# Second sequence's queries and keys prepared sooner and ahead of V, and the last weight part decoded where it was loaded

## The chip, the cores and the metric

The kernel runs on 1 core of a Trainium2 chip. The metric is the device time of one execution in microseconds (us). A core has five engines that work side by side, each through a queue of its own, in order: PE (matmuls), DVE and ACT (elementwise work on vectors), POOL (gathers and some elementwise work) and SP (which issues most DMAs). They wait for each other through semaphores.

## The reference

Block-sparse attention over 4 sequences of 8 heads, 768 tokens and 64 channels, and behind it a feed-forward layer of two matmuls over all 3072 tokens.

```python
mask = np.abs(blk_i - blk_j) <= 1            # blocks of 32 tokens
mask |= (blk_i == 0) | (blk_j == 0) | (blk_i == n_blocks - 1) | (blk_j == n_blocks - 1)
mask |= sampled                              # three random key blocks for each query block
attn = softmax(where(mask, scale * q @ k.T, -1e9))
x = (attn @ v).transpose(0, 2, 1, 3).reshape(B * S, H * D)      # 3072 x 512
h = x @ w_in                                 # 512 x 2048, given as float64
out = np.maximum(0.01 * h, h) @ w_out        # 2048 x 512, given as float64
```

## The kernel before

**Numbers in two halves.** Queries, keys, V, the probabilities, x and the weights are each split into a high and a low float16 half, and products are made from two or three matmuls. Each operand is first scaled by a power of two; for that it is squared and summed (on ACT with `square`, for the weights on PE with `squares`), the sum goes through PE once more (`scale_sum`: rows named q_sum, k_sum, v_sum, wi_sum, wo_sum) and a few small DVE instructions make the scale (`scale_of`).

**Attention.** The work goes in steps, 192 in all: for each of 4 sequences, 3 items of 256 queries, in each 4 tiles of 64 queries, for each tile 4 pairs of heads. Steps 0 to 47 are sequence 0, and step 48 is the first of sequence 1. Names carry these numbers: s_0_2_3_1 is sequence 0, item 2, tile 3, head pair 1, so step 45 (rows of the order leave out the first number in places). A step has scores on PE (`scores`, L714), the masked softmax on DVE and ACT (p, L723 and L735), the probabilities' two halves (pp, `unit_high` on ACT L762, `unit_split` on DVE L783), a transpose by DMA for two pairs together (pt, L788), and the product with V on PE (av, `pair_av`, L815). p has 4 buffers, pp and pt 3 each: pp of a pair can be written once the pair three before has been transposed. Tiles 1 to 11 of a sequence read their sampled keys and values from gathers: `gather_k` copies them out of kt on POOL (kg), and `gather_v` by indirect DMA out of scr, where V's halves are written.

**Side work.** Before a sequence starts, its keys (`prep_k`, four head pairs), V (`prep_v`) and queries (`prep_q`, halves of 128 queries) are prepared. These are generators; `side_step` advances them once a step by a quota, queries first and the others in the order in which they were started. `prep_q` squares on ACT, sums on PE, splits on ACT and DVE (qa), transposes by DMA into qs (L599), and copies qs with its halves swapped into qxs (L601, L602). The first scores of a sequence need qs, qxs and kt of head pair 0. kt has 2 buffers; sequence 1's kt takes the place of sequence 0's.

**Weights.** They are given as float64 and decoded on the chip. They come in 8 parts, w_in and w_out in turn (wi0, wo0, ... wi3, wo3; parts 0 to 7), each of 4 chunks of 128 x 512. `load_w` loads raw words into a free place (`raw_for`); `decode` makes float32 in W from them with one ACT and three DVE instructions (L363 to L367); `finish` squares a part on PE (`squares`, L201), makes its scale and writes the two halves over W (L430 and L435). Parts 6 and 7 go chunk by chunk (groups of one chunk), through three half places in wbuf. Both decode into the last slot of W, so part 7 is decoded only when part 6 has been split, and its own halves go through a temporary in wbuf (L425, L426, L428).

**The feed-forward layer.** h (`ffn_h`, L850) are groups of 24 matmuls, then ACT L856, DVE L859 and L863 and POOL L864 make g, and o (`ffn_o`, L877) are 12 matmuls a group. The first two items go weight part by weight part, as parts come in; the others once all weights are there. From step 48 on h groups are handed out by a table of due steps.

**What sets the order.** A scheduler puts the instructions of each engine into a fixed order, by priorities and by buffers. PE's results of h, of all sums and of all squares share 3 banks of PSUM (`bank`, tag h), taken in the order of the program: what takes a bank early in the program stands early on PE.

Of the kernel before, what the change touches and what calls it, by code (L numbers as in the profile page):

```python
# [12 lines left out]
BF16 = mybir.dt.bfloat16  # L13
F32 = mybir.dt.float32
I32 = mybir.dt.int32
AF = mybir.ActivationFunctionType
# [3 lines left out]
P = 128  # L20
# [39 lines left out]
    "side": 1.2,  # L60
    "side0": 1.6,
    "spair": 1,
    "spread": 8,
# [9 lines left out]
def tile_block_sparse_attention_ffn(  # L73
# [99 lines left out]
    def together(emits):  # L173
# [15 lines left out]
        "p a b c -> p (a b c)").bitcast(F32)[:, :P]  # L189

    def squares(parts, name, fl):

# [3 lines left out]
        pb = bank(f"{name}_sq")  # L196
        blocks = [t.bitcast(BF16).rearrange("p (n l) -> p n l", l=2)[:, c:c + P, 1]
                  for t in parts for c in range(0, t.shape[1], P)]
        begin = len(nc.cur_bb.bb.instructions)
# [119 lines left out]
    wlast = wbuf.bitcast(I32).rearrange("p (c l) -> p c l", l=2)  # L319
    used, busy = {}, set()  # L320
    wtmp = [wbuf[:, WI * i:WI * (i + 1)] for i in range(2)]
    W16 = W.rearrange("p a b c -> p (a b c)").bitcast(F16).rearrange("p (a b l c) -> p a b l c", a=2 * NQ, b=NP, l=2)
# [4 lines left out]
    def raw_for(part, w, n):  # L327

        if w == 1:
            free = [("w", i) for i in range(3)]  # L330
        else:
            free = [a for a in range(4, 2 * NQ) if a >= part + 2 and (
                a == 4 or part and all((0, hp) in kready for hp in range(NP)))] + ["w"]
# [8 lines left out]
        if a == "w":  # L342
            return wlast[:, :2 * WI], keys(a)
        return half(wlast, a[1]) if w == 1 else wraw[a - 4], keys(a)

    def load_w(g):
# [9 lines left out]
        nc.sync.dma_start(out=raw.rearrange("p (c x) l -> p c (x l)", c=g.w), in_=src.bitcast(I32))  # L356
        behind(begin, last_sp.get("p"))

        def decode():
# [15 lines left out]
    def prep_weights():  # L375
# [3 lines left out]
        for n in range(NQ):  # L379
            for k_, kind in enumerate(("wi", "wo")):  # L380
# [4 lines left out]
                for c in range(0, NP, w):  # L385
                    g = Group()
                    g.part, g.w, g.n = i, w, NP * i + c
                    g.d3, g.d16 = W[:, at, c:c + w, :], W16[:, i, c:c + w]
                    g.d = g.d3.rearrange("p c x -> p (c x)")
                    g.src = (w_in[c * P:(c + w) * P, n * WI:(n + 1) * WI] if k_ == 0  # L390
                             else w_out[(n * PER + c) * P:(n * PER + c + w) * P, :])
# [25 lines left out]
        def finish(n, kind, gs):  # L417
            inv, s = scales(squares([g.d for g in gs], f"{kind}{n}", "w"), 1, f"{kind}{n}", keep=f"{kind}{n}", fl="w")
            invs[kind, n] = inv
            yield 1  # L420
            for i, g in enumerate(gs):
                hi, lo = g.d16[:, :, 1, :], g.d16[:, :, 0, :]
                if (n, kind) == (NQ - 1, "wo"):
                    tmp = wtmp[i % 2].unsqueeze(1)
# [21 lines left out]
        for n, kind, gs in parts:  # L446
            for i, g in enumerate(gs):
                load(CFG["ahead"])
# [5 lines left out]
            before = (n, kind, gs)  # L454
            if gs[0].part >= 2 * NQ - 2:
                yield from finish(*before)
                before = None
# [497 lines left out]
    def side_step(amount):  # L955

        quota[0] = min(quota[0] + amount, 2 * amount)
        for key in sorted(flows, key=lambda a: a[0] != "q"):
            if quota[0] <= 0:
# [179 lines left out]
    for u in units:  # L1139
# [5 lines left out]
        if step == 6 or step % 8 == 3 and step > 8:  # L1145
            get_q((step + 5) // 8 + 1)
        if step % 8 == CFG["q_at"] % 8:
            start_q(step // 8 + (2 if CFG["q_at"] < 8 else 1))
        if nb < B:
            g = it.j * 16 + ui  # L1150
            t = g - (CFG["k_at"] if b else CFG["k_at0"])
            every = CFG["k_every"] if b else 5
            if t % every == 0 and 0 <= t // every < NP:
# [26 lines left out]
        for w in CFG["ord1" if step >= CFG["ord1_at"] else "ord"]:  # L1180
# [49 lines left out]
            elif w == "p":  # L1230
                side_step(CFG["side0"] if step < 16 else CFG["side"])
                gather_step(2)
# [83 lines left out]
```

## Time and profile before

| | |
|---|---|
| time, median of 3 runs | 850.7 us (850.25 to 853.37) |
| the profiled execution | 851.52 us |
| its span, first to last instruction | 849.8 us |
| PE busy (share of the span) | 749.3 us (88%) |
| DVE busy | 595.5 us (70%) |
| ACT busy | 507.6 us (60%) |
| POOL busy | 352.8 us (42%) |
| mean granted clock of PE | 0.955 |

Busy time is that of instructions, not of their waits. A row of the timeline has its start, its length in us, the engine, the line, what is written and read, how many instructions were merged, and in brackets how long the engine was idle ahead of it and what ended that. SPq is SP's queue of DMA issues: the length is that of the issue, not of the transfer. PE's granted clock is the share of full clock that the throttle let through.

### The profile page before, as it was taken

How to read it: one execution, taken by the hardware profiler on the slowest of the kernel's cores; microseconds unless marked ns; L12 is line 12 of the kernel's file. 1: busy time of each engine (PE TensorE's matmuls, PEld its weight loads, DVE VectorE, ACT ScalarE, POOL GpSimd, SP SyncE). 2: the span in 40 equal slices, each digit the busy share in tenths (PEclk: the TensorE clock that was granted, in tenths of full speed). 3: DMA queues.
4: the chain of work that ended last, by engine and by line, in shares of the span. 5: the costliest groups of instructions: out<-in, count | busy, mean ns of one | idle time of the engine just before them, and what ended most of it. 6: DMA issues, size and time to landing. Idle time of an engine off the chain costs nothing.

```text
span 849.8 us, 20081 instructions
## 1 busy us (share of the span) xinstructions
PE 749.3 (88%) x7140; PEld 500.6 (59%) x7140; DVE 595.5 (70%) x1595; ACT 507.6 (60%) x1199; POOL 352.8 (42%) x472
## 2 busy tenths in 40 slices
PE   1666675857798999999999999998999999999997
PEld 1455543545465666666666666665666666667664
DVE  5768889898777976867777777678666776651221
ACT  5757678776445766767566667675657556551211
POOL 0218356433233464646343455454244545332221
PEclk9977778989799999999999999999999999999999
DMA  9979289998756999996969999969586766662000
GB/s 198 273 218 247 73 176 240 245 260 147 168 131 106 175 213 190 203 179 146 197 154 154 196 182 186 202 130 204 119 155 150 125 149 139 125 129 35 26 1 25
DMA packets 312004, 135.33 MB, mean 159 GB/s; under 512 B 279774, under 2 KB 292063, under 8 KB 311903
## 3 DMA queue, kind: packets, MB, share of 16 engines
q1 hardware_dynamic: 305262, 113.59, 67.2%
q0 software_dynamic: 6640, 20.45, 9.3%
q8 instruction: 56, 0.92, 0.5%
q14 instruction: 46, 0.37, 0.2%
HBM read 65.58 MB, written 12.58 MB: 92 GB/s over the span
## 4 chain that ended last, share of the span: by engine, by line
PE 70%; DMA 12%; DVE 10%; issue 3%; ACT 2%; SPq 2%; POOL 0%; POOLq 0%; ACTq 0%; DVEq 0%
PE h L850 27%; PE o L877 26%; PE s L714 8%; PE av L815 7%; DMA pt<-pp 3%; DMA wbuf<-in_moe_w_out_dram 2%; DMA qxs_q<-qs_q 2%; DMA qs_q<-qa_q 2%; DVE p L723 2%; DVE pp L783 2%; PE turn L773 2%; DVE W L365 1%; DVE W L435 1%; DVE W L367 1%; PE q_sum L135 1%
## 5 line engine op out<-in xcount | busy, mean ns | idle before, releaser
L877 PE MATMUL o<-W,g 128*128 128x512 f16 x1152 | 270.9, 381 | 6.4 <-DVE ob L898 4.2
L850 PE MATMUL h<-x,W 128*128 128x256 f16 x2304 | 274.2, 277 | 0.2 <-DVE x L833 0.2
L850 PEld LDWEIGHTS <-W 128*128 128x128 f16 x2304 | 225.0, 100 | 37.7 <-issue 3.9
L864 POOL TENSOR_TENSOR g<-ht,g 128x512 f16<-128x512 f32 x96 | 116.9, 1217 | 304.5 <-DVE g L863 254.6
L735 ACT ACTIVATE p<-p,mx 128x384 f32<-128x384 f32 x208 | 126.2, 607 | 158.7 <-DVE mx L723 123.0
L877 PEld LDWEIGHTS <-g 128*128 128x128 f16 x1152 | 108.7, 98 | 125.6 <-issue 10.8
L656 POOL COPY kg<-kt 128x256 f16 x264 | 135.0, 540 | 45.0 <-issue 15.4
L783 DVE SCALAR_TENSOR_TENSOR pp<-p,r,pp 128x384 f16<-128x384 f32 x188 | 120.4, 666 | 24.9 <-ACT pp L762 23.6
L762 ACT ACTIVATE pp<-p,r 128x384 f16<-128x384 f32 x188 | 104.2, 604 | 23.9 <-DVE r L747 10.2
L723 DVE CUSTOM_DVE_ANT_0 p<-s,em,nsc 128x384 f32<-128x384 f32 x176 | 102.0, 608 | 19.8 <-PE s L714 17.1
L683 POOL DMA_INDIRECT vg<-scr,rows x88 | 91.3, 1037 | 50.4 <-issue 20.3
L859 DVE SCALAR_TENSOR_TENSOR ht<-ht 128x512 f32<-128x512 f32 x96 | 67.8, 706 | 53.3 <-ACT ht L856 52.7
L815 PE MATMUL av<-pt,vg 128*64 128x128 f16 x2112 | 82.1, 226 | 10.1 <-DMA pt<-pp 9.6
L815 PEld LDWEIGHTS <-vg 128*64 128x64 f16 x2112 | 73.4, 114 | 27.4 <-issue 21.7
L714 PE MATMUL s<-kg,qs_q 128*64 128x384 f16 x352 | 66.2, 351 | 25.0 <-DVE mx L723 22.7
L856 ACT ACTIVATE ht<-h,gd 128x512 f32<-128x512 f32 x80 | 53.8, 672 | 57.3 <-PE h L850 54.7
L714 PEld LDWEIGHTS <-qs_q 128*64 128x64 f16 x416 | 27.0, 111 | 79.2 <-issue 53.7
L714 PE MATMUL s<-kg,qxs_q 128*64 128x384 f16 x352 | 64.0, 343 | 5.4 <-DMA qxs_q<-qs_q 5.4
L747 DVE RECIPROCAL r<-sum 128x2 f32<-128x2 f32 x96 | 15.4, 161 | 60.2 <-ACT sum L746 57.8
L863 DVE CAST g<-ht 128x512 f16<-128x512 f32 x96 | 41.8, 435 | 9.4 <-PE o L877 7.2
L735 ACT ACTIVATION_READ_ACCUMULATOR p<-p,mx 128x1 f32 x208 | 39.0, 187 | 0.0
L714 PEld LDWEIGHTS <-qxs_q 128*64 128x64 f16 x416 | 26.2, 114 | 20.8 <-DMA qxs_q<-qs_q 9.7
(138 smaller groups left out, 758.0 us busy)
## 6 DMA issues: line engine op xcount, KB each, us to landing
vg<-scr SPq DMA_DIRECT2D x33, 256.0 KB
qxs_q<-qs_q SPq DMA_DIRECT2D x48, 128.0 KB
v<-in_v_dram SPq DMA_DIRECT2D x32, 192.0 KB
scr<-v SPq DMA_DIRECT2D x16, 384.0 KB
W<-in_moe_w_in_dram SPq DMA_DIRECT2D x5, 1024.0 KB
rq<-in_q_dram SPq DMA_DIRECT2D x20, 256.0 KB
out_dram<-ob SPq DMA_DIRECT2D x20, 256.0 KB
rk<-in_k_dram SPq DMA_DIRECT2D x24, 192.0 KB
```

The source lines that it names most:

```text
L656: nc.gpsimd.tensor_copy(out=kg[:, :, slot * BLOCK:(slot + 1) * BLOCK], in_=kt[:, :, bass.ds(off, BLOCK)])
L683: nc.gpsimd.indirect_dma_start(out=vg[:n_, c, :], out_offset=None, in_=scr[b][:, :], in_offset=bass.IndirectOffsetOnAxis(ap=rows[:n_, c - ...
L714: nc.tensor.matmul(o, a, k, start=(n == 0), stop=(n == 1)))
L723: nc.vector.tensor_tensor_reduce(out=u.p[i], in0=u.sp[i], in1=kgs[u.b, u.T][1] if u.T else zero.to_broadcast([P, KEYS]), scale=u.nsc, scal ...
L735: nc.scalar.activation(u.p[i], u.p[i], AF.Exp, scale=-1.0, bias=u.mx[:, :1], accum_out=u.pair.sum[:, u.pi, i:i + 1])
L762: nc.scalar.activation(pp[:, 0, :], p, AF.Copy, scale=u.r)
L783: nc.vector.scalar_tensor_tensor(out=pp[:, 1, :], in0=p, scalar=u.r, in1=pp[:, 0, :], op0=ALU.mult, op1=ALU.subtract)
L815: nc.tensor.matmul(o, a, m, start=(c == 0 and l == 0), stop=(c == n - 1 and l == 1)))
L850: nc.tensor.matmul(c.ph[:, i], w, x, start=(d == 0 and m == 0), stop=(d == NP - 1 and m == 2)))
L859: nc.vector.scalar_tensor_tensor(out=c.t, in0=c.t, scalar=0.01, in1=c.t, op0=ALU.mult, op1=ALU.max)
L864: nc.gpsimd.tensor_tensor(out=c.g[:, 1], in0=c.t, in1=c.g[:, 0], op=ALU.subtract)
L877: nc.tensor.matmul(o, a, w, start=(c.first and i == 0 and m == 0), stop=(c.last and i == 1 and m == 2)))
```

## The change

1. Side work: `side_step` takes queries, then keys, then V. Its quota is 2.0 a step from step 28 to 47 (1.2 before).
2. Sequence 1's keys are loaded and started every 4 steps (5 before), from step 26 on; its first queries are started at step 37 (40 before).
3. Part 7: three of its four groups are decoded in the words where they were loaded, in wbuf, without their own place in W: `decode_here` shifts and joins the low words in place. They are split out of there straight into W's halves, without the temporary. Their load no longer waits for part 6 to be split, and the first of them is decoded between part 6's scale and its split.
4. Part 7's last group is loaded through the first half of the last slot of W, once part 6 has been split from it, and decoded as before.
5. `squares` is given the upper halves of the words (`upper`, or every fourth 16-bit word in place); what is squared is the same.

```diff
+    "side1": 2.0,
...
     def raw_for(part, w, n):
-        if w == 1:
+        if n == last:
+            free = [("s", 0)] if moved[0] else []
+        elif w == 1:
             free = [("w", i) for i in range(3)]
...
+        if n == last:
+            return half(wraw[-1], 0), keys(a)
...
+        def decode_here():
+            lo, hi = raw[:, :, 0], raw[:, :, 1]
+            f = hi.bitcast(F32)
+            nc.scalar.activation(f, f, AF.Copy, scale=2.0 ** -112)
+            nc.vector.tensor_scalar(out=lo, in0=lo, scalar1=29, scalar2=None, op0=ALU.logical_shift_right)
+            nc.vector.scalar_tensor_tensor(
+                out=lo, in0=hi, scalar=3, in1=lo, op0=ALU.logical_shift_left, op1=ALU.bitwise_or)
+            nc.vector.scalar_tensor_tensor(
+                out=lo, in0=hi, scalar=-0x80000000, in1=lo, op0=ALU.bitwise_and, op1=ALU.bitwise_or)
+            g.d3 = lo.bitcast(F32).unsqueeze(1)
+            g.top = raw.rearrange("p c l -> p (c l)").bitcast(BF16).rearrange("p (n l) -> p n l", l=4)[:, :, 1]
+        if g.here:
+            return decode_here
...
+                    g.here = i == 2 * NQ - 1 and c < NP - 1 and w_in.dtype != F32
...
-                if (n, kind) == (NQ - 1, "wo"):
+                if g.n == last or (n, kind) == (NQ - 1, "wo") and not g.here:
...
-            if gs[0].part >= 2 * NQ - 2:
+            if gs[0].part == 2 * NQ - 2:
+                fin = finish(*before)
+                before = None
+                yield next(fin)
+                load(CFG["ahead"])
+                decs.popleft()()
+                yield 2
+                yield from fin
+                moved[0] = True
+            elif gs[0].part == 2 * NQ - 1:
                 yield from finish(*before)
                 before = None
...
-        for key in sorted(flows, key=lambda a: a[0] != "q"):
+        for key in sorted(flows, key=lambda a: "qkv".index(a[0])):
...
-        if step % 8 == CFG["q_at"] % 8:
-            start_q(step // 8 + (2 if CFG["q_at"] < 8 else 1))
+        if step == 37:
+            start_q(6)
+        elif step % 8 == 0 and step != 40:
+            start_q(step // 8 + 1)
...
-            every = CFG["k_every"] if b else 5
+            every = CFG["k_every"] if b else 4
...
-                side_step(CFG["side0"] if step < 16 else CFG["side"])
+                side_step(CFG["side0"] if step < 16 else CFG["side1"] if 28 <= step < 48 else CFG["side"])
```

What it moves. On PE, about the end of sequence 0: before, the sum of sequence 1's first queries (q_0_0_sum, the fourth row) stands behind the squares and the sum of part 7 (wo_sq, wo_sum).

```order
L201 LDWEIGHTS W
L201 MATMUL wo_sq<-W 128x128
L135 MATMUL wo_sum<-wo_ss,ones 128x1
L135 MATMUL q_0_0_sum<-ss_q_0_0_2993,ones 128x1
L850 LDWEIGHTS W
L850 MATMUL h_1_4_3273<-x_1_1979,W 128x256
```

Now, with lines that stand 1 to 37 further down in the file, it stands behind the sum of part 6 (wi_sum) and the tile product av of item 2, tile 1.

```order
L852 LDWEIGHTS vg_100
L852 MATMUL av_2_1_0_3402<-pt_2_1_3_3251,vg_100 64x128
L136 MATMUL wi_sum<-wi_ss,ones 128x1
L136 MATMUL q_0_0_sum<-ss_q_0_0_2742,ones 128x1
L887 LDWEIGHTS W
L887 MATMUL h_0_10_2949<-x_0_999,W 128x256
```

Between the two places lie h_0_10, h_1_0 and h_1_2 and all squares of part 7. Sequence 1's first scores now stand on PE ahead of h_1_4 to h_1_10 and of most of o_1_0 and o_1_4.

On SP, about steps 32 to 36: before, the swapped queries qxs_q_2_1 and the transpose pt_2_0_1 stand ahead of the transpose of sequence 1's first keys (kt from k_k_0).

```order
L599 DMA_TRANSPOSE qs_q_2_1_2480<-qa_q_2_1_2257 128x8x128
L528 DMA rq_0_0_2485<-in_q_dram 32x8x64
L529 DMA rq_0_0_2485<-in_q_dram 32x8x64
L530 DMA rq_0_0_2485<-in_q_dram 64x8x64
L601 DMA qxs_q_2_1_2482<-qs_q_2_1_2480 64x1024
L602 DMA qxs_q_2_1_2482<-qs_q_2_1_2480 64x1024
L356 DMA wbuf<-in_moe_w_in_dram 128x1024
L542 DMA rk_2_2572<-in_k_dram 128x6x64 x2
L788 DMA_TRANSPOSE pt_2_0_1_2582<-pp_2_0_0_2378 128x12x128
L574 DMA_TRANSPOSE kt_2387<-k_k_0_2093 128x12x128
```

Now the keys' transpose stands ahead of all of these.

```order
L636 DMA_TRANSPOSE qs_q_2_1_2485<-qa_q_2_1_2267 128x8x128
L565 DMA rq_0_0_2490<-in_q_dram 32x8x64
L566 DMA rq_0_0_2490<-in_q_dram 32x8x64
L611 DMA_TRANSPOSE kt_2344<-k_k_0_2029 128x12x128
L638 DMA qxs_q_2_1_2487<-qs_q_2_1_2485 64x1024
L639 DMA qxs_q_2_1_2487<-qs_q_2_1_2485 64x1024
L567 DMA rq_0_0_2490<-in_q_dram 64x8x64
L366 DMA wbuf<-in_moe_w_in_dram 128x1024
L825 DMA_TRANSPOSE pt_2_0_1_2593<-pp_2_0_0_2387 128x12x128
```

The keys' transpose moved up, past qxs_q_2_1, one raw load of weights and pt_2_0_1; it waits, as before, for the last gather of old keys on POOL.

More of the change, by code (lines that the diff above doesn't have):

```diff
@@ L189, in tile_block_sparse_attention_ffn, with upper @@
         "p a b c -> p (a b c)").bitcast(F32)[:, :P]
+    def upper(t):
+        return t.bitcast(BF16).rearrange("p (n l) -> p n l", l=2)[:, :, 1]
     def squares(parts, name, fl):
@@ L196, in squares @@
         pb = bank(f"{name}_sq")
-        blocks = [t.bitcast(BF16).rearrange("p (n l) -> p n l", l=2)[:, c:c + P, 1]
-                  for t in parts for c in range(0, t.shape[1], P)]
+        blocks = [t[:, c:c + P] for t in parts for c in range(0, t.shape[1], P)]
         begin = len(nc.cur_bb.bb.instructions)
@@ L320, in tile_block_sparse_attention_ffn @@
     used, busy = {}, set()
+    last = 2 * NQ * NP - 1
+    moved = [False]
     wtmp = [wbuf[:, WI * i:WI * (i + 1)] for i in range(2)]
@@ L389, in prep_weights @@
                     g.d = g.d3.rearrange("p c x -> p (c x)")
+                    g.top = upper(g.d)
+                    g.here = i == 2 * NQ - 1 and c < NP - 1 and w_in.dtype != F32
                     g.src = (w_in[c * P:(c + w) * P, n * WI:(n + 1) * WI] if k_ == 0
@@ L417, in finish @@
         def finish(n, kind, gs):
-            inv, s = scales(squares([g.d for g in gs], f"{kind}{n}", "w"), 1, f"{kind}{n}", keep=f"{kind}{n}", fl="w")
+            inv, s = scales(squares([g.top for g in gs], f"{kind}{n}", "w"), 1, f"{kind}{n}", keep=f"{kind}{n}", fl="w")
             invs[kind, n] = inv
@@ L446, in prep_weights @@
         for n, kind, gs in parts:
-            for i, g in enumerate(gs):
+            for i, g in enumerate(gs[1:] if gs[0].part == 2 * NQ - 1 else gs):
                 load(CFG["ahead"])
```

## The prediction

> **What bounds the kernel now.** I read the page first, its slices of busy time, then stretches of the span (the windows).
>
> ```profile
> span 849.8 us, 20081 instructions
> PE   1666675857798999999999999998999999999997
> DVE  5768889898777976867777777678666776651221
> PEclk9977778989799999999999999999999999999999
> 151.00:193.00 42.00, 29.34 (x328) 19.66 (x325) 38.93 (x98) 33.17 (x78) 17.73 (x22) 0.91 1.11 253
> 151.00:246.50 95.50, 73.71 (x711) 50.09 (x708) 80.17 (x210) 60.45 (x128) 33.34 (x35) 0.91 0.92 198
> 246.50:304.00 57.50, 52.65 (x489) 32.45 (x489) 47.88 (x132) 36.66 (x93) 24.97 (x41) 0.97 0.75 147
> 304.00:849.80 545.80, 534.56 (x5141) 355.32 (x5140) 345.41 (x915) 310.42 (x753) 235.51 (x308) 1.00 0.71 142
> ```
>
> A slice is 21.2 us. In a window's row stand its length, the busy time of PE, PEld, DVE, ACT and POOL, then the granted clock, the DMA share and GB/s. From 304 us on PE is busy for 534.56 of 545.80 us at full clock: that part is as long as its matmuls. The change leaves PE's order alike from its row 4102 on (some 320 us), so the end moves by what PE loses ahead of there. From 151 to 246.5, the second half of sequence 0 and the way into sequence 1, PE works for 73.71 us of 95.5 and DVE for 80.17: DVE is the fuller engine, and the room is here. Next I read PE in order of time, with its waits in brackets (the last row is from ACT).
>
> ```profile
> 149.35 4.03 PE L850 MATMUL h<-x,W 128*128 128x256 f16 x24
> 153.22 1.08 PE L201 MATMUL wi_sq<-W 128*128 128x128 bf16 x16
> 154.23 0.35 PE L714 MATMUL s<-kg,qs_q 128*64 128x384 f16 x2
> ...
> 192.86 0.33 PE L714 MATMUL s<-kg,qxs_q 128*64 128x384 f16 x2
> ...
> 225.66 0.40 PE L201 MATMUL wo_sq<-W 128*128 128x128 bf16 x4 [1.37 <-DVE W L367]
> 227.19 0.58 PE L135 MATMUL wo_sum<-wo_ss,ones 128*128 128x1 f32 x2 [1.14 <-DVE wo_ss L204]
> 227.64 0.56 PE L135 MATMUL q_sum<-ss_q,ones 128*128 128x1 f32 x2
> ...
> 237.13 5.42 PE L850 MATMUL h<-x,W 128*128 128x256 f16 x48
> 242.38 3.62 PE L877 MATMUL o<-W,g 128*128 128x512 f16 x16
> 245.93 0.35 PE L714 MATMUL s<-kt,qs_q 128*64 128x384 f16 x2
> ...
> 173.41 0.62 ACT L230 ACTIVATE qa_q<-rq 128x512 f16<-128x512 f32 x1
> ```
>
> The last scores of sequence 0 end at 193, the first of sequence 1 begin at 245.93. Its first queries were squared on ACT at 173.41, but their sum (q_sum) stands on PE behind the squares and the sum of weight part 7, which come at 225.66 and 227.19. That is 54 us of standing in the queue, and the reason for the change.
>
> **What the change moves, and the break-even.** With the new order q_sum comes right behind part 6's sum (wi_sum), ahead of three h groups that it stood behind and of all squares of part 7. So the first scores come sooner; but what PE did ahead of them is not gone. By the order, four h groups (h_1_4 to h_1_10) and 38 o matmuls (40 of o_1_0 and o_1_4 stood ahead, now 2) go behind the first scores, and 24 av matmuls (0.9 us) come ahead. At full clock an h group is 5.42/2 = 2.71 us, an o matmul 3.62/16 = 0.226 us: 4 x 2.71 + 38 x 0.226 - 0.9 = 18.5 us. From 246.5 to 304 PE was nearly full (52.65 of 57.5), so moved work finds 5 us of gaps at most. Hence the test: the change gains only if the first scores begin ahead of 245.9 - 18.5 = 227.4 us, and each us earlier or later is about a us at the end.
>
> **When they can begin.** I take DVE, whose queue is in order and holds all the softmax.
>
> ```profile
> 155.16 0.61 DVE L723 CUSTOM_DVE_ANT_0 p<-s,em,nsc 128x384 f32<-128x384 f32 x1
> 179.28 0.61 DVE L723 CUSTOM_DVE_ANT_0 p<-s,em,nsc 128x384 f32<-128x384 f32 x1
> 225.72 1.15 DVE L508 SCALAR_TENSOR_TENSOR v<-v,v_s,v 128x384 f16<-128x384 f32 x2
> 233.68 0.74 DVE L426 SCALAR_TENSOR_TENSOR W<-W,wo_s,wbuf 128x512 f16<-128x512 f32 x1
> 234.34 0.28 DVE L428 COPY W<-wbuf 128x512 f16<-128x512 f16 x1
> 235.26 0.68 DVE L859 SCALAR_TENSOR_TENSOR ht<-ht 128x512 f32<-128x512 f32 x1
> 236.79 0.42 DVE L863 CAST g<-ht 128x512 f16<-128x512 f32 x1
> ```
>
> Start: h_0_4 (4.03) and the squares of part 4 (1.08) no longer stand ahead of the scores of step 32, so its first softmax comes at about 155.2 - 4.1 = 151.1. Of DVE's 80.17 us, these leave the stretch ahead of the first softmax of sequence 1: two V pairs with their halves (2 x 1.15), part 7's four splits and copies (4 x 0.74 + 4 x 0.28), three ht and g (3 x 1.1), and some 20 small ones (2.7, at 0.13 each); one x and xf come in (0.8): 11.6 us. So 68.6 us stay, and without any idle the first softmax is at 219.7, the scores 0.7 earlier, at 219. That is one end. With all the idle that DVE has there today (95.5 - 80.2 = 15.3) it is 234.3, the other end.
>
> Which waits go, which stay, and what is new:
>
> ```profile
> DVE pp L783 <- ACT pp L762: 3.4, 1, 3.4
> DVE W L364 <- ACT W L363: 2.5, 2, 2.4
> DVE ht L859 <- ACT ht L856: 2.0, 1, 2.0
> DVE k_tot L149 <- PE k_sum L135: 1.7, 1, 1.7
> ...
> 190.11 1.12 ACT L762 ACTIVATE pp<-p,r 128x384 f16<-128x384 f32 x2 [0.87 <-DMA pt<-pp]
> 204.09 1.12 ACT L762 ACTIVATE pp<-p,r 128x384 f16<-128x384 f32 x2 [3.94 <-DMA pt<-pp]
> ...
> 165.03 1.25 SPq L599 DMA_TRANSPOSE qs_q<-qa_q  x1
> 168.25 0.58 SPq L601 DMA_DIRECT2D qxs_q<-qs_q  x1
> 172.54 2.88 SPq L788 DMA_TRANSPOSE pt<-pp  x1
> 175.53 2.12 SPq L574 DMA_TRANSPOSE kt<-k_k  x1
> 185.07 1.56 SPq L788 DMA_TRANSPOSE pt<-pp  x1
> 192.92 17.69 SPq L788 DMA_TRANSPOSE pt<-pp  x3
> ```
>
> (A row of waits: us in total, times, longest.) Three of these go: the wait for ht and that for k_sum belong to the 20 us before the first scores, in which DVE had nothing else, and the one for the raw load of part 7 (W L364) goes because three of its four groups are decoded while scores still run. The 3.4 us for pp I keep: pp waits for a tile that a transpose must have read, and bulk loads stay beside it.
>
> New is a place on SP. The transpose of the new keys (kt) moves up in front of the two qxs copies of q_2_1, a raw load and the transpose pt_2_0_1, and it waits for the last gather of old keys on POOL, whose place it takes over. Queued behind it are all of these; DVE waits for pt_2_0_1 in pp_2_1_2, which now stands ahead of the softmax of step 40, not behind it. When? SP comes free after q_2_1's transpose at 166.3; the change puts 384 KB more of keys ahead of that, at the 253 GB/s of 151 to 193 some 1.5 us, so 167.8; two rq issues, two qxs, an rq and a raw load (six at 0.58, as the qxs row) with kt (2.1) and pt itself (2.9) end at 176.3, and it lands 3.5 us later (as from 185.07 + 1.56 to 190.11): 179.8. DVE's list up to there I estimate from the order: 8 softmax at 0.61 (4.9), 14 rows of pp, x and kg at 0.42 to 0.57, as L863 and half of L508 (7.0), four pieces of 512 columns of decoding at three rows of about 0.6 (7.1), low halves of keys and queries with small rows (3.6). That is 22.6 us, so it stands there at 173.7: 6.1 us of waiting. Bounds: nothing, if DVE is late or SP early; 12 us, if pt lands as late as the one issued at 192.92, which let ACT go at 204.09.
>
> Sum: 219 + 6.1 + 3.4 = 228.5, against the break-even of 227.4: 1.1 us lost. The profiled execution took 851.52 us (span 849.8 and 1.7 around it), the median is 850.7; I put the difference on the median: 851.8.
>
> The other edits. Side work at 2.0 a step for 1.2, and keys every 4 steps for 5, add nothing: the same instructions come earlier, and their price is the place on SP above and k_1's sum on PE, which pulls h_0_4 and part 4 behind itself; that is in the sum through DVE's list. V after K: V's copies to scr go behind the queries' transpose on SP; the first tile of sequence 1 reads V in SBUF, and scr is read only from the second on, so nothing. The last group of part 7 now waits, on SP, for part 6's second split, one DVE row ahead of the queries' own last row, so it holds the queries' transpose by 0.7 us at most. Decoding in place: as many DVE instructions, on every second word; three copies (L428, 0.8 us) go. The shift (L364) was on packed words.
>
> ```profile
> L365 DVE SCALAR_TENSOR_TENSOR W<-wbuf,W 128x512 int32<-128x512 int32 x8 | 6.3, 793 | 0.1
> L364 DVE TENSOR_SCALAR W<-W 128x512 int32<-128x512 int32 x8 | 3.3, 429 | 2.5 <-ACT W L363 2.5
> ```
>
> On every second word it costs between this, 429 ns, and the op beside it with two operands, 793: at most 3 x 0.36 = 1.1 us, and I take half, which cancels with the copies. [...]
>
> **The rivals.** *Faster: DVE never waits.* If pt_2_0_1 lands before DVE gets there, and the pp wait goes since the raw loads of part 7 are spread further apart, the first scores come between 219 and 223: 4.4 to 8.4 us gained, about 844.5. For it: DVE was busy for 23 of the 24.1 us between the two softmaxes quoted. Against: SP is as late today. *Slower: SP holds the transposes.* Two raw loads of part 7 now follow each other on SP ahead of pt_2_1_1, and the second waits for the decode of part 6's third group, which DVE reaches after the softmax of step 40. All transposes of steps 36 to 47 stand behind. Each 512 KB takes 2 us at 253 GB/s; a transpose that lands 11 us after its issue, as at 192.92, instead of 3.5, twice, makes the first scores 234 to 238, 7 to 10 us lost: about 859. It decides from 12.6 us of DVE idle between the softmax of step 32 and the first of sequence 1. The rows of 192.92 and 204.09 speak for it, the fewer key loads left by then against it. [...] *It doesn't do what it says:* the queries are ready but held on SP, and the first scores stay near 240; then 12 us of the moved work are lost, 863. Only one DVE row lies between, so I give it little.
>
> **How the numbers follow.** About 0.5%, 4.25 us, is what a measurement of this kernel can tell from no change. Forecast (no change that can be told, 847 to 855): 0.41. Faster: 0.32. SP holds: 0.22, not as said: 0.05, together 0.27 slower. The range leaves out half of each outer case's tail: 843.5 (bound 842.3) to 858.5 (where the slower rival begins is 857).
>
> **What would show it.** Right: first scores of sequence 1 at 225 to 231 and PE full behind them; a DVE wait of 4 to 8 us for pp ahead of step 40's softmax; more PE idle from 151 to 193 than now. Wrong: first scores ahead of 223, or behind 232; or PE gaps of more than 6 us between them and row 4102, since then the break-even is no measure.

## The result and the profile after

The kernel after is slower: 851.91 us median of 22 runs (843.23 to 863.39) against 844.66 us of 22 runs of the kernel before (834.52 to 853.37). The ratio is 1.0093 with a 95% interval of 1.0066 to 1.0119, some 7.9 us. A second measurement of the unchanged kernel after (e6 below) gave 1.0125 (1.0064 to 1.0185). The ratios leave disturbed executions out, so they need not be the quotient of two medians. The three runs of before that the prediction started from, 850.25 to 853.37, lie at the upper end of what its 22 runs show.

The page of the kernel after, to be read against the rows of before:

```profile
span 844.1 us, 20063 instructions
PE   1566675478989999999999999999999999999997
PEclk9977986689999999999999999999999999999999
```

This span is 5.7 us shorter than that of before, though the medians say the opposite. So one execution of each is not enough to compare whole spans, and the changed stretch must be cut out. PE's order is the same in both kernels up to the sum of item 2's second queries (q_2_1_sum) and again from row 4103 of PE's order on (its 2211th matmul). The sum is at 149.14 us in before and at 144.94 here, and the time from row 4103 to the end is 524.8 us and 522.6: both differ without any difference in PE's order. What the change does lies between. The windows of the kernel before, from that sum on, first 27.2 us (as far as k_sum in the kernel after) and then the whole stretch (length, then busy time of PE, PEld, DVE, ACT and POOL, granted clock, DMA share, GB/s):

```profile
149.14:176.34 27.20, 20.00 (x200) 12.69 (x201) 24.42 (x55) 19.77 (x45) 15.86 (x19) 0.94 1.10 238
149.14:325.03 175.89, 149.24 (x1415) 98.09 (x1416) 144.84 (x389) 110.40 (x253) 68.02 (x86) 0.93 0.90 182
```

The same windows of the kernel after:

```profile
144.94:172.14 27.20, 10.37 (x110) 7.31 (x110) 21.23 (x52) 20.22 (x53) 10.38 (x18) 0.63 1.11 242
144.94:321.48 176.54, 149.36 (x1416) 100.00 (x1416) 148.63 (x392) 113.60 (x261) 66.46 (x87) 0.91 0.89 183
```

In the first 27 us PE works for 10.4 us instead of 20.0, at a granted clock of 0.63 instead of 0.94. The whole stretch is 0.65 us longer. A second execution of each kernel (e5 and e6) widens this to 8.6 us:

```profile
144.84:172.04 27.20, 20.77 (x200) 12.83 (x201) 25.90 (x59) 21.58 (x52) 14.72 (x19) 0.91 1.11 244
144.84:316.91 172.07, 150.32 (x1416) 98.03 (x1416) 148.27 (x393) 112.36 (x260) 66.18 (x86) 0.93 0.89 186
```

That is before; and after:

```profile
143.29:170.49 27.20, 10.98 (x116) 7.67 (x117) 22.73 (x57) 20.93 (x54) 11.13 (x18) 0.56 1.11 242
143.29:324.00 180.71, 152.14 (x1416) 101.01 (x1416) 150.13 (x394) 114.49 (x262) 68.16 (x87) 0.89 0.87 178
```

The first profile of before was a late execution: its stretch took 175.9 us, the second 172.1, and the parts ahead and behind were 4.3 and 2.7 us longer too. The means of the two pairs are 174.0 and 178.6, 4.6 us apart. Of this 3.7 us is PE's idle time (stretch less busy: 26.7 and 21.8 before, 27.2 and 28.6 after) and the rest PE's longer busy time.

Where PE is idle tells more. PE of the kernel after, in order of time, with its waits in brackets:

```profile
144.71 0.59 PE L136 MATMUL q_sum<-ss_q,ones 128*128 128x1 f32 x2
145.23 0.85 PE L751 MATMUL s<-kg,qs_q 128*64 128x384 f16 x4
...
156.02 0.53 PE L751 MATMUL s<-kg,qs_q 128*64 128x384 f16 x2 [2.92 <-DVE pp L820]
...
165.22 1.49 PE L852 MATMUL av<-pt,vg 128*64 128x128 f16 x24 [6.43 <-DMA pt<-pp]
...
172.19 0.59 PE L136 MATMUL k_sum<-ss_k,ones 128*128 128x1 f32 x2 [4.84 <-ACT k_k L233]
172.64 4.58 PE L887 MATMUL h<-x,W 128*128 128x256 f16 x24
...
182.43 2.78 PE L887 MATMUL h<-x,W 128*128 128x256 f16 x24
...
223.54 0.52 PE L751 MATMUL s<-kt,qs_q 128*64 128x384 f16 x4 [0.40 <-DMA qs_q<-qa_q]
...
227.21 0.52 PE L751 MATMUL s<-kt,qxs_q 128*64 128x384 f16 x4 [0.89 <-DMA qxs_q<-qs_q]
...
247.27 0.35 PE L751 MATMUL s<-kt,qs_q 128*64 128x384 f16 x2 [2.54 <-DMA kt<-k_k]
```

In the kernel before, h_0_4 ran right behind the first row, at 149.35 of its own clock. Here it runs 27.9 us after that row, behind the sum of sequence 1's second keys (k_sum at 172.19), and with it wi2_sq, h_0_6 and o_0_4, which were what PE had to do while it waited for softmax and p's transpose. The waits are now bare: 2.7 (at 149.41, not shown), 2.9, 6.4 and 4.8 us. The granted clock is lower beside them, 0.63 against 0.94 in these windows: a group of 24 h matmuls takes 4.58 us here, at a granted clock of 0.59, and another 2.78 ten us later, at 1.00.

Split in three, PE's idle time reads so, in us, for the four profiles of the two kernels (before and e5 are the kernel before, after and e6 the kernel after):

| part of the stretch | before | e5 | after | e6 |
|---|---|---|---|---|
| first 27.2 us | 7.2 | 6.4 | 16.8 | 16.2 |
| from there to sequence 1's first scores | 14.6 | 11.0 | 5.2 | 5.5 |
| from the first scores to row 4103 | 4.9 | 4.3 | 5.2 | 6.9 |

The first row has 9.7 us more idle time in the kernel after (means of two profiles), the second 7.5 less, the third 1.5 more. The second row is no proof that the sooner queries gain: the 9.7 us of work that left the first row runs behind it, and that alone can fill holes there.

### The profile page after: what moved, and what is told of

It is laid out like the page before. It is cut to its first block, busy times and chain, and to the rows that moved or that the text cites. A ratio compares the mean times of both kernels' runs of the same rounds, so it can differ in the third digit from the quotient of the medians.

```text
span 844.1 us, 20063 instructions
## 1 busy us (share of the span) xinstructions
PE 745.2 (88%) x7140; PEld 499.6 (59%) x7140; DVE 593.3 (70%) x1592; ACT 508.2 (60%) x1199; POOL 349.8 (41%) x472
## 4 chain that ended last, share of the span: by engine, by line
PE 69%; DVE 11%; DMA 11%; ACT 4%; issue 2%; SPq 2%; POOL 0%; POOLq 0%; ACTq 0%; DVEq 0%
PE h L887 27%; PE o L914 26%; PE s L751 7%; PE av L852 6%; DMA kt<-k_k 2%; DMA pt<-pp 2%; DVE p L760 2%; DMA scr<-v 1%; DVE pp L820 1%; DMA wbuf<-in_moe_w_out_dram 1%; PE turn L810 1%; DMA qxs_q<-qs_q 1%; DMA kt<-W 1%; DVE W L391 1%; DMA vg<-scr,rows 1%
## 5 line engine op out<-in xcount | busy, mean ns | idle before, releaser
L693 POOL COPY kg<-kt 128x256 f16 x264 | 132.0, 527 | 45.9 <-PE s L751 21.9
L820 DVE SCALAR_TENSOR_TENSOR pp<-p,r,pp 128x384 f16<-128x384 f32 x188 | 119.7, 665 | 21.8 <-ACT pp L799 20.5
L852 PE MATMUL av<-pt,vg 128*64 128x128 f16 x2112 | 84.5, 228 | 17.3 <-DMA pt<-pp 7.2
L852 PEld LDWEIGHTS <-vg 128*64 128x64 f16 x2112 | 75.6, 116 | 35.5 <-issue 25.9
```

The costliest lines, as they stand in the source:

```text
L693: nc.gpsimd.tensor_copy(out=kg[:, :, slot * BLOCK:(slot + 1) * BLOCK], in_=kt[:, :, bass.ds(off, BLOCK)])
L820: nc.vector.scalar_tensor_tensor(out=pp[:, 1, :], in0=p, scalar=u.r, in1=pp[:, 0, :], op0=ALU.mult, op1=ALU.subtract)
L852: nc.tensor.matmul(o, a, m, start=(c == 0 and l == 0), stop=(c == n - 1 and l == 1)))
```

## The experiments

Theory K, formed from these rows: the loss is the place of the second keys' sum, k_1_sum (k1_1_sum with the sequence), ahead of h_0_4, the squares of part 4 and h_0_6. Its rivals were W (the prediction's slower case: part 7's raw loads on SP hold p's transposes), Q (earlier queries gain nothing, since PE's work only moves behind the first scores) and, for the later runs, S (the larger side quota and earlier loads cost by themselves).

All ratios are to the kernel before, timed on the same chip in the same rounds. "Stretch" and "PE idle" are of one profiled execution each, from q_2_1_sum to PE's row 4378, behind which the order is the same in all twelve kernels; by this measure before has 190.2 us with 26.7 idle, and after 190.7 with 27.2. The profiled execution of e7 was 5.6 us faster than its median, those of e1 and e10 were the slowest of their six, so small differences of these two columns say little by themselves.

| kernel | what it has of the change | median us | ratio (95%) | stretch | PE idle |
|---|---|---|---|---|---|
| e5 | nothing (before again) | 844.09 | 1.0024 (0.9981 to 1.0067) | 186.3 | 21.8 |
| e6 | all (after again) | 851.81 | 1.0125 (1.0064 to 1.0185) | 194.8 | 28.6 |
| e1 | in-place decode only | 856.0 | 1.0137 (1.0083 to 1.0191) | 200.2 | 30.0 |
| e2 | all but the decode | 848.1 | 1.0045 (1.0007 to 1.0082) | 189.1 | 25.2 |
| e3 | queries at step 37 only | 863.7 | 1.0208 (1.0137 to 1.0279) | 203.5 | 37.7 |
| e4 | order q-k-v, queries, decode | 846.65 | 1.0023 (0.9989 to 1.0056) | 191.2 | 24.3 |
| e7 | all, second keys later | 844.05 | 0.9992 (0.9944 to 1.0041) | 186.5 | 19.3 |
| e8 | order, quota, queries | 849.41 | 1.0086 (1.0043 to 1.013) | 192.1 | 26.2 |
| e9 | order, quota | 854.69 | 1.0086 (1.0035 to 1.0137) | 193.3 | 29.6 |
| e10 | order, quota, second keys sooner | 860.21 | 1.0159 (1.0117 to 1.0202) | 208.8 | 41.4 |
| e11 | e7 without the decode | 848.28 | 1.0039 (1.0007 to 1.0071) | 189.0 | 23.8 |
| e12 | e7, fourth keys later | 846.47 | 0.9999 (0.9963 to 1.0035) | 187.0 | 20.0 |

**e1, the decode alone.** The kernel after with the other four edits undone:

```diff
-        for key in sorted(flows, key=lambda a: "qkv".index(a[0])):
+        for key in sorted(flows, key=lambda a: a[0] != "q"):
-    "side1": 2.0,
+    "side1": 1.2,
-            every = CFG["k_every"] if b else 4
+            every = CFG["k_every"] if b else 5
-        if step == 37:
-            start_q(6)
-        elif step % 8 == 0 and step != 40:
-            start_q(step // 8 + 1)
+        if step % 8 == CFG["q_at"] % 8:
+            start_q(step // 8 + (2 if CFG["q_at"] < 8 else 1))
```

> The kernel before with the in-place decode of part 7 and the early load of its last group alone; the order of flows, the side quota, the keys' interval and the queries' step stay as before. Theory K (the keys pulled forward cost the time: PE waits for the sum of sequence 1's second keys ahead of h_0_4 and the squares of part 4): no loss, ratio to before 0.995 to 1.003, since k_1_sum stands behind h_0_6 as before. Rival W (part 7's raw loads on SP hold the transposes of steps 36 to 47): slower, ratio 1.005 to 1.010, DVE waits for pp of 5 us or more between 175 and 200 us. Rival Q (starting the queries sooner only moves PE work behind the first scores and gains nothing for it): 0.997 to 1.003, since they are not sooner here.

1.0137: it costs even more than W said, but not by W's wait. From 175 to 200 us this is all that DVE waits for:

```profile
DVE W L390 <- ACT W L389: 0.2, 1, 0.2
```

Late in the stretch PE waits for another sequence-1 item's queries, 3.78 us:

```profile
312.66 0.85 PE L751 MATMUL s<-kg,qxs_q 128*64 128x384 f16 x4 [3.78 <-DMA qxs_q<-qs_q]
```

That is one of several small waits (30.0 us idle against 21.8 and 26.7). As much of the longer stretch is busy time: 170.2 us, against 164.5 and 163.5 in the two profiles of before, at a granted clock of 0.94, 0.89 and 0.90 in three windows from 242.2 to 337.5 us, against 1.00, 0.94 and 1.00 in three from 239.1 us on in before and the same three values from 234.8 us on in e5. I did not isolate why the decode alone brings this. K did not foresee a loss here either.

**e2, all but the decode.** The kernel before with the four edits that e1 undoes.

> The kernel after without the in-place decode: queries, keys, V in that order, side quota 2.0 from step 28 to 47, keys every 4 steps, queries at step 37; part 7 decoded as before. Theory K: the loss stays, ratio to before 1.006 to 1.012, with PE waits for k_sum of 3 us or more between 155 and 180 us, ahead of h_0_4. Rival W: the loss is gone, 0.992 to 1.002, since part 7's loads wait for part 6's split again. Rival Q: 1.004 to 1.010.

1.0045 lies between K and W. The wait for k_sum that K named is there (3.5 us at 170), and so is the one for p's transpose (5.6 us at 164). By this pair of kernels the decode costs some 0.5% where the keys are early.

**e3, the queries alone.**

```diff
-        if step % 8 == CFG["q_at"] % 8:
-            start_q(step // 8 + (2 if CFG["q_at"] < 8 else 1))
+        if step == 37:
+            start_q(6)
+        elif step % 8 == 0 and step != 40:
+            start_q(step // 8 + 1)
```

> The kernel before with one edit: sequence 1's first queries are started at step 37 instead of 40. By PE's order their sum then stands right behind part 6's sum, as in the kernel after, and the first scores ahead of most of part 7's squares; k_1_sum stays behind h_0_6. Theory K: the first scores come at about 225 us and the time is 0.990 to 0.999 of before. Rival W: the same, 0.990 to 0.999. Rival Q: no gain or a loss, 1.000 to 1.008, with PE gaps between the first scores and 304 us growing by as much as the scores come sooner.

The largest loss of all, 1.0208, outside every expectation. PE of this kernel:

```profile
205.55 0.49 PE L714 MATMUL s<-kt,qs_q 128*64 128x384 f16 x4
...
212.11 0.35 PE L714 MATMUL s<-kt,qs_q 128*64 128x384 f16 x2
...
240.95 0.28 PE L135 MATMUL k_sum<-ss_k,ones 128*128 128x1 f32 x2
...
256.82 0.53 PE L714 MATMUL s<-kt,qs_q 128*64 128x384 f16 x2 [7.77 <-DMA kt<-k_k]
```

The first scores come 62.9 us behind q_2_1_sum, earliest of all kernels, and the second pair at 212. Then they stop: the third keys' sum stands at 241 and their transpose holds PE for 7.8 us at 257. A tile needs all four pairs of keys; with the queries alone only the first two are early. So the early queries need the early keys beside them. Whether the steps of one of these keys cost the kernel after its time is what e7 asks.

**e4, keys and quota as before.** The kernel after with side1 at 1.2 and the keys every 5 steps.

> The kernel after with the side quota back at 1.2 and the keys back at every 5 steps; the flows' order, the queries at step 37 and the in-place decode stay. By PE's order k_1_sum is behind h_0_6 and part 5's first squares again, as before. Theory K: the loss is gone, ratio 0.990 to 1.000. Rival W: it stays, 1.005 to 1.012. Rival Q: 1.000 to 1.008.

1.0023: most of the loss has gone with k_1_sum back behind h_0_6, but the gain that K allowed did not come; the number lies in Q's range, not in K's. The quota went back in the same edit.

**e5 and e6, the two kernels again.**

> The kernel before, unchanged, a second profiled execution, and timed against itself as a measure of the noise. Stretch from the sum of q_2_1 to PE's row 4103: 175.9 us in the first profile. Theory K+ (the kernel after loses in its median execution what its one profile did not show, or the first profile of before was a late one): 168 to 174 us here if the first profile of before was late, 174 to 178 if it was a common one. Ratio 0.997 to 1.003 by any theory.

> The kernel after, unchanged, a second profiled execution. The same stretch took 176.5 us in the first profile, 0.7 more than in before, where the medians differ by 7. Theory K+: 179 to 185 us, with more than 11 us of PE waits for the transpose of p and for k_sum between 150 and 175 us (11.2 in the first profile); or, if before's profile was the late one, 175 to 178 again. Ratio to before 1.006 to 1.012.

Both stretches came as K+ had them: 172.1 and 180.7 us (their rows are above). The ratios are 1.0024, inside its range, and 1.0125, just above it. The waits in e6, 6.8 us for p's transpose and 3.1 for k_sum, are 9.9, less than the 11 that I named.

**e7, the second keys later: the test of K.** The kernel after with one pair of keys moved, load by one step and start by two, to where the kernel before has them:

```diff
-            if t % every == 0 and 0 <= t // every < NP:
-                get_k(nb, t // every)
-            if t % every == every - 2 and 0 <= t // every < NP:
-                start_k(nb, t // every)
+            gets = [every * c for c in range(NP)] if b else [0, 5, 8, 12]
+            starts = [every * c + every - 2 for c in range(NP)] if b else [2, 8, 10, 14]
+            if t in gets:
+                get_k(nb, gets.index(t))
+            if t in starts:
+                start_k(nb, starts.index(t))
```

> The kernel after with one edit: sequence 1's second keys are loaded one step later and started two steps later, where they were in the kernel before; keys 2 and 3, the queries and everything else stay at the new steps. By PE's order h_0_4, the squares of part 4 and h_0_6 stand ahead of k_1_sum again, and the first scores stand where they do in the kernel after. Theory K (k_1's sum ahead of this work is what costs): the loss is gone, ratio to before 0.992 to 1.001, PE waits for k_sum and for the transpose between 150 and 175 us under 4 us. Rival W (part 7's loads hold SP): 1.006 to 1.012 as after. Rival S (the rest: side quota, earlier key loads fill the DMA engines by any order): 1.003 to 1.010.

0.9992: the loss is gone, 7.8 us less than e6 in the median. On SP the edit also puts the first keys' transpose back behind qxs_q_2_1, and one of the two raw loads that W blames behind pt_2_1_1, so W rests on the rows of the kernel after (below) and on e10, not on this run. The windows of this kernel:

```profile
142.61:169.81 27.20, 20.92 (x198) 12.72 (x199) 26.82 (x58) 20.54 (x47) 14.82 (x20) 0.90 1.00 223
169.81:216.77 46.96, 34.60 (x326) 25.69 (x325) 40.98 (x116) 32.81 (x72) 11.30 (x10) 0.77 0.98 216
216.77:314.97 98.20, 97.51 (x893) 61.39 (x893) 78.87 (x215) 58.29 (x139) 39.92 (x58) 0.97 0.85 161
142.61:314.97 172.36, 153.03 (x1417) 99.80 (x1417) 146.68 (x387) 111.63 (x257) 66.04 (x86) 0.91 0.91 186
```

and its PE:

```profile
142.82 3.53 PE L887 MATMUL h<-x,W 128*128 128x256 f16 x24
148.88 2.78 PE L887 MATMUL h<-x,W 128*128 128x256 f16 x24
...
173.09 0.59 PE L136 MATMUL k_sum<-ss_k,ones 128*128 128x1 f32 x2 [2.09 <-ACT k_k L233]
...
216.77 0.85 PE L751 MATMUL s<-kt,qs_q 128*64 128x384 f16 x4 [3.50 <-DMA qs_q<-qa_q]
```

PE has its 20.9 us of work back in the first 27, h_0_4 and h_0_6 stand in the waits again, k_sum costs 2.1 us instead of 4.8 and 3.1, and the first scores come at 74.2 us behind q_2_1_sum against 78.6 and 80.8. So the second keys' steps are what costs the kernel after its time.

How they cost it is less plain than K has it. Split as in the table above, PE's idle time in e7 is 6.3, 12.4 and 0.7 us. Against the kernel after (means 16.5, 5.4 and 6.1) that is 10.2 less in the first part, 7.0 more in the second and 5.4 less behind the first scores. The holes of the first 27 us come back for the most part in the second part; the largest share of what e7 saves in its profile lies behind the first scores, where the kernel after waits 2.5 us for a transpose of keys (its row of 247.27 above, 2.9 us in e6) and e7 has no wait above 0.4 us. And the scores are not sooner at no price: 97.5 us of PE's work stand behind them up to row 4103, against 92.8 and 93.0 in the kernel after.

**e8, no decode and keys every 5.** The kernel after with both undone; order, quota and queries stay.

> The kernel after without the in-place decode and with the keys at every 5 steps: the flows' order, the side quota of 2.0 and the queries at step 37 stay. k_1_sum stands behind h_0_6 as before, the first scores ahead of all squares of part 7, and the second keys' sum comes soon after V's. Theory K, with the decode as a second loss of some 0.5% (from the two kernels with and without it): faster than before, 0.988 to 0.998. Rival: what the early queries gain is lost again by the 18 us of FFN work behind them, 0.998 to 1.004.

A miss on both sides, 1.0086. In PE's order h_0_4, part 4's squares and h_0_6 stand ahead of k_1_sum as in before, so K's loss is absent. The first scores come 65.2 us behind q_2_1_sum, and then the last keys are late, as in e3: their sum stands 97.6 us behind, the fourth pair's scores 108.4.

**e9 and e10, K on another base.** e9 is the kernel before with the flows' order and the quota; e10 has e9's second keys one step sooner in load and two in start, with this over e9:

```diff
+            gets = [every * c for c in range(NP)] if b else [0, 4, 10, 15]
+            starts = [every * c + every - 2 for c in range(NP)] if b else [2, 6, 13, 18]
```

(and the two calls as in e7; the first keys start one step sooner too, at 2 instead of 3).

> The kernel before with the flows' order and the side quota of 2.0 from step 28 to 47; keys every 5 steps, queries at step 40, part 7 decoded as before. k_1_sum stands behind h_0_6 as before and q_0_0_sum behind part 7's sum. It is the base for the next kernel. Theory K: 0.996 to 1.004 of before, stretch 171 to 176 us. Rival S (the larger quota itself loads the engines or the DMA wrongly): 1.005 or more.

> The kernel of e9 with one edit: sequence 1's second keys are loaded one step sooner and started two steps sooner, as in the kernel after; nothing else of the change. By PE's order k_1_sum then stands ahead of h_0_4, the squares of part 4 and h_0_6. Theory K: 0.5 to 1.2 % slower than e9 (4 to 10 us), with PE idle of 14 us or more in its waits over 2 us between 145 and 175 us, for p's transpose and for k_sum among them. Rival: within 0.3 % of e9, if that loss needs the early queries or the in-place decode beside it.

e9 is no neutral base: 1.0086, as S said, though e9 has the flows' order beside the quota and does not tell the two apart. With V and keys pulled forward, PE stands 6.36 us in front of part 7's squares, which wait for DVE's decode, and the first queries' sum stands behind these:

```profile
215.03 0.61 PE L202 MATMUL wo_sq<-W 128*128 128x128 bf16 x4 [6.36 <-DVE W L368]
```

e10 is slower again, 1.0159 against 1.0086: 0.7% (5.5 us in the medians), inside K's 0.5 to 1.2, though the intervals of the two ratios overlap (1.0035 to 1.0137 and 1.0117 to 1.0202). The windows of e10 and its PE:

```profile
147.18:174.38 27.20, 10.80 (x110) 7.51 (x110) 21.63 (x52) 20.31 (x54) 11.56 (x18) 0.56 1.18 212
147.18:339.55 192.37, 150.99 (x1415) 98.51 (x1416) 150.40 (x394) 113.50 (x262) 66.66 (x89) 0.87 0.86 169
```

```profile
170.04 1.49 PE L816 MATMUL av<-pt,vg 128*64 128x128 f16 x24 [8.64 <-DMA pt<-pp]
...
176.90 0.85 PE L715 MATMUL s<-kg,qxs_q 128*64 128x384 f16 x4 [4.73 <-DMA qxs_q<-qs_q]
...
185.16 0.59 PE L136 MATMUL k_sum<-ss_k,ones 128*128 128x1 f32 x2 [5.20 <-ACT k_k L231]
185.61 4.23 PE L851 MATMUL h<-x,W 128*128 128x256 f16 x24
```

The same picture of the first 27 us as in the kernel after, made by the keys without early queries and without the decode: 10.8 us of work in the first 27, h_0_4 behind k_sum, the clock at 0.56. It is not as clean a cut as e7: the first keys start a step sooner too, and 4.7 us of the waits are for swapped queries, whose copies stand behind a load of keys on SP here.

**e11, e7 without the decode.**

> The kernel of e7 (second keys later) without the in-place decode: part 7 decoded as before. If the decode costs what the two pairs hint (some 0.5 %), 0.990 to 0.997 of before; if it is needed to bring part 7's squares ahead of the first scores' softmax, slower than e7: 1.002 to 1.010.

1.0039, beside 0.9992 with the decode; the intervals overlap. In its one profile PE waits 6.63 us for a p of sequence 1, behind the first scores:

```profile
246.14 2.77 PE L816 MATMUL av<-pt,v 128*64 128x128 f16 x48 [6.63 <-DMA pt<-pp]
```

So the decode's sign depends on the order around it: a loss alone (e1) and with early keys (after against e2), no loss and perhaps a gain here.

e11 is also e2 with the second keys later, the very edit of e7 over the kernel after, and here it gains nothing: 1.0039 against e2's 1.0045 (each to before on its own chip). The first 27 us and the stretch to row 4103, e2 and then e11:

```profile
143.66:170.86 27.20, 12.14 (x117) 8.62 (x118) 22.68 (x59) 20.47 (x54) 11.55 (x18) 0.50 1.11 244
143.66:318.60 174.94, 149.76 (x1415) 100.05 (x1416) 147.74 (x395) 112.96 (x262) 66.99 (x86) 0.89 0.88 184
```

```profile
144.92:172.12 27.20, 21.25 (x198) 12.74 (x199) 26.90 (x59) 21.32 (x50) 14.59 (x20) 0.88 1.02 225
144.92:319.83 174.91, 151.12 (x1417) 100.62 (x1417) 146.11 (x392) 113.24 (x261) 67.25 (x86) 0.90 0.90 184
```

e2 has K's holes, with PE at work for 12.1 us of the first 27 against 21.3, and its stretch is as long as that of e11. So K does not hold by itself: without the decode the later rows take up all that the first 27 us lose.

**e12, the fourth keys later.** e7 with `[0, 5, 8, 16]` for the loads and `[2, 8, 10, 19]` for the starts.

> The kernel of e7 with sequence 1's fourth keys loaded four steps later and started five steps later. In e7 ACT waited 4.2 us at 204 us for the place of these keys (k_k behind the transpose kt), with part 6's split and the first queries behind it in its queue, and PE 3.5 us for the queries at 217. If that wait is what is late next, the first scores come 2 to 4 us sooner than in e7 and the time is 0.993 to 0.998 of before; if the fourth keys are then late for their scores, 1.000 to 1.006.

ACT's wait of 4.2 us has gone and the queries are split 3.5 us sooner, 65.6 us behind q_2_1_sum against 69.1:

```profile
214.25 0.70 ACT L631 ACTIVATE qa_q<-rq,q_s 128x512 f16<-128x512 f32 x1
214.86 0.83 ACT L233 ACTIVATE k_k<-rk 128x768 f16<-128x768 f32 x1
```

But the first scores come at 77.6 us, not sooner: by PE's order more FFN work stands ahead of them. The stretch, 187.0 us, is that of e7 and e5, and the time that of before, 0.9999. No kernel here beats the one before by more than its interval; e7 and e12 equal it. So Q stands in them: e7 has its first scores at 74.2 us where the two profiles of before have 96.8 and 93.5, and gains nothing by it.

## Why the prediction was right or wrong

The number forecast was no change, 851.8 us, against 850.7 then measured; the kernel is 0.93% slower. So a difference that the forecast put at 1.1 us was 7 to 8. That 851.9 us lies on the number forecast is chance: the first three runs of before, on which it was put, were 6 us slower than the median of its 22. Step by step:

*PE's unchanged tail.* Right: row 4103 to the end took 524.8 and 522.1 us in before, 522.6 and 522.0 in after.

*The break-even of 18.5 us.* Right as a sum. PE's busy time from the first scores to row 4103, in before and then after:

```profile
245.93:325.03 79.10, 74.25 (x702) 46.87 (x702) 62.82 (x174) 50.50 (x127) 35.26 (x52) 0.98 0.85 160
```

```profile
223.54:321.48 97.94, 92.76 (x818) 59.40 (x818) 80.34 (x217) 58.87 (x139) 43.28 (x58) 0.98 0.80 159
```

92.76 - 74.25 is 18.5 us, and PE's gaps there are 5.2 and 6.9 us. Wrong was what it was taken from: the first scores of before came 96.8 us behind q_2_1_sum in the profile shown, 93.5 in the second. From the second the break-even is 75.0, and the first scores of the kernel after, at 78.6 and 80.8, lie 3.6 and 5.8 us beyond it. The gap of 6.9 us in the second profile is above the 6 us at which the prediction itself called the break-even no measure.

*The first scores at 228.5.* Right in sum, by errors that cancel. On the clock of before's profile they came at 149.1 + 78.6 = 227.7 and at 229.9. Between step 32's first softmax and sequence 1's first, DVE was busy for 69.1 us in both profiles (I had 68.6) and idle for 10.3 and 11.6 (I had 9.5). But it began 1.9 and 3.0 us later than I had it, and the first softmax came 4.6 and 4.8 us behind the first scores, not 0.7, since the scores with the swapped queries came 3.7 us behind the others.

*Where DVE waits.* Wrong. Neither the wait of 6.1 us for pt_2_0_1 nor that of 3.4 is there. DVE of the kernel after, ahead of step 40's softmax:

```profile
172.81 0.16 DVE L150 TENSOR_SCALAR k_tot<-k_sum 128x1 f32<-128x1 f32 x1 [3.22 <-PE k_sum L136]
...
174.60 1.02 DVE L607 SCALAR_TENSOR_TENSOR k_k<-rk,k_s,k_k 128x768 f16<-128x768 f32 x1 [1.01 <-ACT k_k L605]
...
177.25 0.43 DVE L390 TENSOR_SCALAR W<-W 128x512 int32<-128x512 int32 x1 [1.62 <-ACT W L389]
...
180.10 0.61 DVE L760 CUSTOM_DVE_ANT_0 p<-s,em,nsc 128x384 f32<-128x384 f32 x1
```

It waits for the keys and for PE, not for SP. Two wrong waits and their true ones add to about the same.

*"Their price is ... k_1's sum on PE, which pulls h_0_4 and part 4 behind itself; that is in the sum through DVE's list."* This is the step that failed. I saw that h_0_4 moved, booked it as a gain of 4.1 us for the first softmax of step 32 (2.2 us came, counted from q_2_1_sum, in both pairs of profiles), and put the price of the keys' steps on PE at nothing, since PE had room. The price is there: with the second keys back at their old steps (e7) 1.3% of the time goes against e6, and on e9 the sooner steps cost 0.7% (e10). What the rows show of how is this: PE's room was in holes, which h_0_4, part 4's squares, h_0_6 and o_0_4 had filled, and the kernel after has 9.7 us more idle in the first 27 us (means of the two profiles), of which the later rows give 6.0 back. That these holes are the loss is not shown: most of the idle time that e7 saves lies behind the first scores, and e2 has the same holes and takes no longer than e11, which has not.

*"Side work at 2.0 a step ... add nothing."* Wrong where the queries' sum is late, at least together with the flows' order: e9 has these two alone and loses 0.9%, with a new wait of 6.4 us in front of part 7's squares. In e7 both are there without loss.

*The slower rival.* The loss that it named came about (7 to 10 us), its mechanism did not. Its point of decision, 12.6 us of DVE idle, was not reached. ACT, which must have p's transposes read before it writes pp again, waited hardly at all from 151 to 193 us in the kernel after:

```profile
ACT pp L799 <- DMA pt<-pp: 1.2, 2, 0.7
```

although two raw loads stand ahead of those transposes on SP:

```profile
183.11 3.10 SPq L366 DMA_DIRECT2D wbuf<-in_moe_w_out_dram  x2
186.26 4.65 SPq L825 DMA_TRANSPOSE pt<-pp  x2
```

And e10 has the loss without these loads being early.

*The decode in place.* I took the middle of 429 and 793 ns for the shift on every second word. The mean of three is near the far end (L374, against L390 on packed words):

```profile
L374 DVE TENSOR_SCALAR wbuf<-wbuf 128x512 int32<-128x512 int32 x3 | 2.3, 763 | 0.0
...
L390 DVE TENSOR_SCALAR W<-W 128x512 int32<-128x512 int32 x3 | 1.2, 414 | 0.0
```

But the three took 1.39, 0.42 and 0.48 us (at 189.44, 193.10 and 200.09), and in e1 they took 0.42, 0.42 and 0.41. So the shift stood at the near end but for one row, 1.39 in e6 too (at 188.99); what makes that one long is not shown. Against 414 ns each the three are 1.0 us more, a small term.

**What stays open.** The two pairs of profiles give 4.6 us of the 7 to 8 that the medians show; whether the rest is the spread of executions or a term outside the stretch, two profiles of each can't tell. Why the second keys' steps cost 1.3% with the decode (e6 against e7), 0.7% on e9 and nothing between e2 and e11 is open, and so is why the decode alone costs 1.4%. The parts do not add: the decode, the queries, and order with quota lose 1.4, 2.1 and 0.9% alone, and all together, with the second keys in their old place, lose nothing.

## What to carry to other kernels

When an order moves work out of a stretch in which an engine waits, price the holes that it filled, and then look whether later holes take the work up: of 9.7 us lost here 6.0 came back in the kernel after, and between e2 and e11 all of it. A sum whose input is not there yet, put ahead of ready work on an in-order engine, opens a hole by its own wait (4.8 us at k_sum in the kernel after) and others by what it pushes out of the earlier ones (6.4 us at p's transpose there); only the whole stretch tells what that costs. And before a small difference is argued from one profile, cut the stretch that differs and hold it against a second execution of the same kernel: here that alone moved the break-even by 3.3 us.

## What the runs showed of the hardware

- The shift on every second 32-bit word took 1.39, 0.42 and 0.48 us for 128x512 in the kernel after and 0.42, 0.42 and 0.41 in e1, against a mean of 0.41 for three on packed words in the kernel after (180 to 250 us).
- PE's granted clock over the first 27.2 us behind q_2_1_sum was 0.50 to 0.63 in the four profiles with 10 to 12 us of PE work there (after, e6, e2, e10), against 0.80 to 0.94 in eight others, with 20 to 23 (before, e1, e3, e5, e7, e9, e11, e12). Right behind that stretch 24 matmuls of 128x256 took 4.58 us in the kernel after at a granted clock of 0.59, ten us later 2.78 at 1.00.
- The kernel before's executions spread over 18.9 us (834.5 to 853.4), and the part ahead of the change, alike in PE's order in all kernels, ended at 142.6 to 152.2 us in twelve profiles (e7 the earliest, e1 the latest).
